# Pooled attention with a SiLU layer behind it: attention work in four groups per tile instead of five, and a second Strassen unit in tile 1

## Chip, cores and metric

The kernel runs on one core of one Trainium2 chip. The metric is the device time of one execution in microseconds. Before the change the median of three runs is 280.44 us (280.3 to 280.5). The profiled execution took 280.58 us; its span, from the first to the last instruction, is 278.7 us at a mean granted TensorE clock of 0.998. All moments below are microseconds from the start of that span.

## What is computed

```python
# q, k, v: 8 batches x 8 heads x 576 tokens x 64
k_p = k.reshape(B, H, Sp, 8, D).mean(axis=3)      # 72 pooled keys per head
v_p = v.reshape(B, H, Sp, 8, D).mean(axis=3)
scores = np.matmul(q, k_p.transpose(0, 1, 3, 2)) / np.sqrt(D)
attn = np.exp(scores - scores.max(-1, keepdims=True))
attn = attn / (attn.sum(-1, keepdims=True) + 1e-09)
x = np.matmul(attn, v_p)                          # -> 4608 tokens x 512
h = x @ w_in                                      # 512 -> 2048
out = (h / (1.0 + np.exp(-h))) @ w_out            # 2048 -> 512
```

## The kernel before

The 4608 tokens are worked off in nine tiles of 512 tokens (t = 0 to 8). Each tile has an "up" part (x by `w_in`, then SiLU) and a "down" part (the result by `w_out`). Attention for batch t + 1 is woven into the down part of tile t, in three visits (0, 1, 2), each a third of the batch's tokens. Each visit has three steps: scores with their exponentials, denominators, and numerators.

Fillers are pieces of other work that are put into the stream of matmuls at given steps:

```python
def spread(fillers, n):
    todo = sorted(fillers, key=lambda f: f[0])
    for i in range(n):
        yield i                                   # one matmul of the main stream is issued
        while todo and todo[0][0] <= i:
            todo.pop(0)[1]()
```

PSUM has eight banks: three under the tag `mm`, five under the tag `at`.

```python
banks = dict(mm=3, at=5)

def scores(b, segs):                              # four "at" banks, then four Exp on ScalarE
    sc = [ps_tile([128, 512], FP32, "at", "sc_ps")[:SP, :w] for s in range(4)]
    for g, i0, i1, cs in seg_cols(segs):
        for c in range(2):
            for s in range(4):
                nc.tensor.matmul(sc[s][:, cs], lhsT=kz[...], rhs=st["qT"][...],
                                 start=(c == 0), stop=(c == 1))
    for s in range(4):
        nc.scalar.activation(es[:, s, :], sc[s], func=AF.Exp, scale=score_scale)

def denominators(b, segs, on_dve=False):          # one "at" bank
    den_ps = ps_tile([128, 512], FP32, "at", "den_ps")
    for s in range(4):
        nc.tensor.matmul(den_ps[32*s : 32*(s+1), :w], lhsT=ones, rhs=es[:, s, :], ...)
    # ... (a variant on VectorE is left out)
    nc.scalar.activation(lnd, den_ps[:, :w], func=AF.Ln)
    nc.scalar.activation(rec, lnd, func=AF.Exp, scale=-1.0)

def numerators(b, segs, tags=("at", "at")):       # one bank of each tag named
    for c in range(2):
        nu_ps = ps_tile([128, 512], FP32, tags[c], "nu_ps")
        # 16 matmuls of vp by es
    for c in range(2):
        nc.vector.tensor_mul(out=xT[...], in0=nu[c][...], in1=rec[...])
```

The up part mixes plain groups (four matmuls of 512 columns into one `mm` bank, then Silu) with units after Strassen: seven products 1 to 7, each of four matmuls of 256 columns, in place of four plain groups. A unit has banks P and Q (`at`) and R (`mm`).

```python
# inside up():  y is the unit
if n == "2":   product(y, 2, "P", True);  nc.scalar.copy(r_sb, ps[y, "P"])
elif n == "5": product(y, 5, "Q", True);  tt(out=rr_sb, in0=ps[y, "Q"], in1=r_sb, op=ALU.add)
elif n == "1": product(y, 1, "R", True);  tt(out=t_sb, in0=ps[y, "R"], in1=rr_sb, op=ALU.subtract)
elif n == "4": product(y, 4, "P", False); hidden(y, 1, 0, ps[y, "P"])      # Silu on ScalarE
elif n == "3": product(y, 3, "Q", False); hidden(y, 0, 1, ps[y, "Q"])
elif n == "7": product(y, 7, "P", False); tt(out=c_sb[0], in0=ps[y, "P"], in1=t_sb, op=ALU.add)
elif n == "6": product(y, 6, "Q", False); tt(out=c_sb[1], in0=ps[y, "Q"], in1=t_sb, op=ALU.add)
elif n == "h": hidden(y, 0, 0, c_sb[0])
else:          hidden(y, 1, 1, c_sb[1])                                    # "s"
```

The down part of tiles 1 to 8 is one such scheme of 7 x 16 = 112 matmuls of 256 columns with three `mm` banks P, Q, R. Its order is: half of product 2, half of 5, the rest of 2, the rest of 5 (steps 0 to 31), then products 1, 4, 3, 7, 6 of 16 steps each. R is read out after product 1.

```python
ps = {n: ps_tile([128, 2, CQ], FP32, "mm", f"o_ps{n}") for n in "PQR"}
# ...
product(1, 0, KQ, cc)
tt(out=t_sb[:, cs], in0=ps["R"][:, cs], in1=rr_sb[:, cs], op=sub)
product(4, 0, KQ, cc)
copy = nc.vector.tensor_copy if last else nc.scalar.copy
copy(o_sb[1][:, cs, LO], ps["P"][:, cs])
# ... products 3, 7, 6
```

Where the attention steps stand in the down part (a = t + 1 is the batch, B = 8):

```python
sc_at, den_at, nu_at = (1, 31, 75), (31, 56, 97), (56, 97, 101)      # t > 0
for n, sg in enumerate(visits):
    f_down.append((den_at[n], lambda sg=sg: denominators(a, sg)))
    f_down.append((sc_at[n], lambda sg=sg: scores(a, sg)))
for n, sg in enumerate(visits):
    if n < 2 or not 0 < t < B - 2:
        f_down.append((nu_at[n], lambda sg=sg: numerators(a, sg)))
    if n == 0 and 1 < t < B - 1:
        f_down.append((nu_at[n], lambda: numerators(a - 1, visits[2])))
```

So numerators 2 already stood in the next tile. Tile 0 has a plain down part of 64 matmuls of 512 columns, with fillers of its own: the sums that pool `v` of batch 1 (VectorE) at steps 20 and 30, and the selection of pooled `v` (TensorE) at steps 37 and 40. The loads that it waits for are issued by GpSimd in this order: `w_out` chunks 0, 1, 2, then `v` of batch 1 in three pieces, then `w_out` chunk 3.

Of the kernel before, what the change touches and what calls it, by code (L numbers as in the profile page):

```python
# [27 lines left out]
FP32 = mybir.dt.float32  # L28
# [8 lines left out]
def kernel(  # L37
# [9 lines left out]
    nc = tc.nc  # L47

    B, H, S, D = q.shape
# [11 lines left out]
    KQ, NQ, CQ = KG // 2, NTT // 2, d_model // 2  # L61
# [29 lines left out]
    def ps_tile(shape, dtype, tag, name):  # L91
        return psum.tile(shape, dtype, tag=tag, bufs=banks[tag], name=name)
# [16 lines left out]
    o_sb = [singles.tile([128, 2, d_model], FP32, name=f"o_sb{n}") for n in range(2)]  # L109
# [130 lines left out]
    def load_slots(eng, b, name, i0, i1, half=None):  # L240
        es = slice(0, RE) if half is None else slice(half * RE // 2, (half + 1) * RE // 2)
        src = (k if name == "k" else v)[b].rearrange("h (sp p) d -> (h sp) (p d)", p=POOL)
        src = src[:, es]
        how = dict(accum_op=ALU.add) if half else {}
        tiles = row_tiles[name]
        w = es.stop - es.start
        if i0 == SLOTS:
            eng.dma_start(
                out=tiles[1][:REST, SLOTS - SA, :w], in_=src[128 * SLOTS :], **how
            )  # L250
        else:
            j = i0 // SA
            eng.dma_start(
                out=tiles[j][:, i0 - SA * j : i1 - SA * j, :w],
                in_=src[128 * i0 : 128 * i1].rearrange("(i r) e -> r i e", r=128), **how
            )
# [145 lines left out]
    def moe_tables():  # L402
        nc.scalar.preload_act_table_set("silu_and_others")
# [38 lines left out]
    def unit_x_sum(t, n):  # L442
        a, b = U_X[n]
        nc.vector.tensor_tensor(
            out=x_sum[:, U_XI[n]], in0=x_quarter(t, *a), in1=x_quarter(t, *b),
            op=ALU.subtract if n in (3, 4) else ALU.add,
        )
# [139 lines left out]
    LO, HI, FULL = slice(0, CQ), slice(CQ, 2 * CQ), slice(0, 2 * CQ)  # L587
# [30 lines left out]
    PW = 4  # L618
# [13 lines left out]
    def down_quarters(t, fillers, last=False):  # L632
        step = spread(fillers, 7 * 2 * KQ)
        ps = {
            n: ps_tile([128, 2, CQ], FP32, "mm", f"o_ps{n}") for n in "PQR"
        }
        bank = {2: "P", 5: "Q", 1: "R", 4: "P", 3: "Q", 7: "P", 6: "Q"}
        begun = set()

        def product(n, k0, k1, cs=(0, 1)):  # L640
            b = bank[n]
            for kt in range(k0, k1):
                for c in cs:
                    next(step)
                    nc.tensor.matmul(  # L645
                        ps[b][:, c, :], lhsT=left(n, kt, c), rhs=W_OUT[n][:, kt, :],
                        start=b not in begun,
                        stop=kt == k1 - 1, skip_group_check=True,
                    )
                    begun.add(b)  # L650

        add, sub = ALU.add, ALU.subtract
        tt = nc.vector.tensor_tensor
        KA = KQ // 2
        product(2, KA, KQ)
        product(5, KA, KQ)
        product(2, 0, KA)
        nc.scalar.copy(r_sb, ps["P"])
        product(5, 0, KA)
        tt(out=rr_sb, in0=ps["Q"], in1=r_sb, op=add)  # L660
        for cc in ((0,), (1,)) if last else ((0, 1),):
            cs = slice(cc[0], cc[-1] + 1)
            product(1, 0, KQ, cc)
            tt(out=t_sb[:, cs], in0=ps["R"][:, cs], in1=rr_sb[:, cs], op=sub)
            product(4, 0, KQ, cc)
            copy = nc.vector.tensor_copy if last else nc.scalar.copy
            copy(o_sb[1][:, cs, LO], ps["P"][:, cs])
            tail = last and cc == (1,)
            if tail:
                store(t, 3, LO, (nc.gpsimd,))  # L670
            product(3, 0, KQ, cc)
            nc.vector.tensor_copy(out=o_sb[0][:, cs, HI], in_=ps["Q"][:, cs])
            if tail:
                store(t, 1, HI)
            product(7, 0, KQ, cc)
            tt(out=o_sb[0][:, cs, LO], in0=ps["P"][:, cs], in1=t_sb[:, cs], op=add)
            for c in cc:
                store(t, c, LO if tail else FULL, (nc.scalar if tail else nc.sync,))
            product(6, 0, KQ, cc)
            tt(out=o_sb[1][:, cs, HI], in0=ps["Q"][:, cs], in1=t_sb[:, cs], op=add)  # L680
            for c in cc:
                if tail:
                    store(t, 3, HI, both)
                else:
                    store(t, 2 + c, FULL, (nc.gpsimd if last else nc.sync,))
        for _ in step:
            pass
# [41 lines left out]
    def load_w_out(c):  # L729
        cs = slice(c * KG // 4, (c + 1) * KG // 4)  # L730
        nc.gpsimd.dma_start(out=w_out_sb[:, cs, :], in_=w_out_r[:, cs, :])
# [43 lines left out]
    for c in range(3):  # L775
        load_w_out(c)
    load_slots(nc.gpsimd, 1, "v", 0, 3)
    load_slots(nc.gpsimd, 1, "v", 3, 4)
    load_slots(nc.gpsimd, 1, "v", 4, 5)
    load_w_out(3)  # L780

    def load_half_2(name, half):
        for i0, i1 in ((0, SA), (SA, SLOTS), (SLOTS, SLOTS + 1)):
# [9 lines left out]
    for t in range(NT):  # L793
        a = t + 1
        f_up, f_down = [], []
        if t == 0:
            GA = 11
            items = [(g, 0, HS) for g in range(GA)]
            items += [(g, HS, NTT - HS) for g in range(GA)]
            items += [(g, 0, NTT) for g in range(GA, KG)]  # L800
            f_up += [(1, lambda: denominators(0, part(0, 1), on_dve=True))]
            f_up += [(5, lambda: denominators(0, part(1, 1), on_dve=True))]
            f_up += [(13, lambda: numerators(0, part(0, 1)))]
            f_up += [(17, lambda: numerators(0, part(1, 1)))]
        else:
            G = lambda *gs: [(g, 0, NTT) for g in gs]
            if t == 1:
                items = (
                    G(12, 13, 14, 15) + [(0, "251")] + G(8) + [(0, "43")] + G(9)
                    + [(0, "7h6")] + G(10) + [(0, "s")] + G(11, 0, 1, 2, 3)  # L810
                )
            else:
                items = []
                for it in THREE[t // B].split():
                    items += [(("BCA".index(it[0])), it[1])] if it[0] in "ABC" else G(int(it[1]))
            if t == 1:
                for n in U_X:
                    f_up.append((0, lambda n=n: unit_x_sum(t, n)))
            for n in (2, 5):
                h_at = 50 if t == B else 54 if t > 1 else 45  # L820
                f_up.append((h_at, lambda n=n: hidden_sum(n, 4, 8)))
            f_up.append((56, lambda: hidden_sum(6, 4, 8)))
            for n, k0 in ((2, 0), (5, 0), (1, 4), (1, 0)):
                f_up.append((64, lambda n=n, k0=k0: hidden_sum(n, k0, k0 + 4)))
            f_down.append((33, lambda: hidden_sum(7, 0, 8)))
            f_down.append((71 if t < B else 50, lambda: hidden_sum(6, 0, 4)))

        for n, t0, f_to, at, parts in (
            (1, 0, f_down, 48, (0, PW)), (3, 0, f_down, 52, (0, PW)),
            (4, 1, f_up, 38, (0, PW)), (7, 1, f_up, 42, (0, PW)),  # L830
            (6, 1, f_up, 60, (0, PW)),
        ):
            for i in range(*parts):
                if t == t0:
                    f_to.append((at + i, lambda n=n, i=i: weight_sum(n, i)))
        if a < B:
# [44 lines left out]
            f_down.append((0, attn_tables))  # L881

            if t:
                sc_at, den_at, nu_at = (1, 31, 75), (31, 56, 97), (56, 97, 101)
            else:
                sc_at, den_at, nu_at = (1, 16, 30), (16, 30, 44), (44, 55, 56)
            for n, sg in enumerate(visits):
                f_down.append((den_at[n], lambda sg=sg: denominators(a, sg)))
                f_down.append((sc_at[n], lambda sg=sg: scores(a, sg)))

            for n, sg in enumerate(visits):
                if n < 2 or not 0 < t < B - 2:
                    f_down.append((nu_at[n], lambda sg=sg: numerators(a, sg)))
                if n == 0 and 1 < t < B - 1:
                    f_down.append((nu_at[n], lambda: numerators(a - 1, visits[2])))
        if 0 < t < B:
            for n in (4, 1, 3, 7, 6):
                f_down.append((98 if t < B - 1 else 44, lambda n=n: unit_x_sum(t + 1, n)))
        if t == 1:
            def unit_weight_tiles():  # L900
                k_w = big.tile([128, 4, 2, 256], BF16, tag="k_raw2", name="w_sum12")
# [3 lines left out]
            f_down.append((72, unit_weight_tiles))  # L905
            for i, n in enumerate(U_W):
                f_down.append((73 if i < 2 else 81, lambda n=n: unit_weight_sum(2, n)))
        moe_tables()
        up(t, f_up, items)
        if t == 0:  # L910
            down(t, f_down, [(0, 1, 2), (3,)])
# [30 lines left out]
```

The softmax here doesn't subtract the row's maximum and nothing guards it: scores larger than these inputs give would overflow.

## Time and profile before

| what | before |
|---|---|
| time, median of 3 | 280.44 us |
| span of the profiled run | 278.7 us |
| TensorE busy | 273.3 us |
| VectorE busy | 218.7 us |
| ScalarE busy | 188.4 us |
| GpSimd busy | 98.7 us |
| tile 1, from its first matmul to that of tile 2 | about 50.9 to 81.2 us |
| DMA, mean | 135 GB/s |

A busy time is the sum of the stretches in which an engine worked on something. Engines work beside each other, so the busy times don't add up to the span; an engine that is nearly always busy sets the time, and work of another engine counts only where that one waits for it. In the views quoted below PE is TensorE, PEld its loading of weights, DVE VectorE, ACT ScalarE and POOL GpSimd; L340 is line 340 of the kernel; `x16` counts instructions; and square brackets tell how long the engine had been idle and what ended that.

### The profile page before, as it was taken

The page shows a single profiled execution, that of the slowest core. Times are in us where ns is not written, and L with a number is a line of the kernel's source. Part 1 is how long each engine was busy: PE and PEld are TensorE (multiplying, and loading weights), DVE is VectorE, ACT ScalarE, POOL GpSimd, SP SyncE. Part 2 cuts the span into 40 slices and gives each one's busy share as a digit, 9 for nine tenths or more (in the row PEclk, how much of TensorE's full clock was granted, in tenths as well). Part 3 has the DMA queues.
Part 4 walks back from the last instruction along what each step waited for, and adds up shares of the span by engine and source line. Part 5 has one row for each costly group of instructions (what it writes and reads, how often), then busy time and mean ns, then how long its engine had stood idle before and what let it go on. Part 6 is the DMA issues. An engine that isn't in the chain of part 4 may idle for free.

```text
span 278.7 us, 7121 instructions
## 1 busy us (share of the span) xinstructions
PE 273.3 (98%) x2865; PEld 201.9 (72%) x2865; DVE 218.7 (78%) x413; ACT 188.4 (68%) x366; POOL 98.7 (35%) x104
## 2 busy tenths in 40 slices
PE   7999999999999999999999999999999999999995
PEld 4348444556778677867888788687877778788784
DVE  4986737889998976897689768986888588966983
ACT  1688765668577966797679757985799478326700
POOL 8745217242148430953086107961630000000001
PEclk9999999999999999999999999999999999999999
DMA  7999999896669887568865845599620041005004
GB/s 198 291 251 249 206 322 190 232 188 118 135 88 216 204 118 145 139 175 123 149 141 150 122 70 133 137 130 134 138 55 2 2 107 46 0 12 141 1 7 146
DMA packets 31312, 37.70 MB, mean 135 GB/s; under 512 B 10352, under 2 KB 22256, under 8 KB 31280
## 3 DMA queue, kind: packets, MB, share of 16 engines
q0 software_dynamic: 23920, 27.03, 52.8%
q1 hardware_dynamic: 6928, 9.58, 12.3%
q10 hardware_dynamic: 432, 0.66, 0.9%
q8 instruction: 22, 0.36, 0.6%
q14 instruction: 10, 0.08, 0.1%
HBM read 36.70 MB, written 9.44 MB: 166 GB/s over the span
## 4 chain that ended last, share of the span: by engine, by line
PE 81%; DMA 12%; POOL 2%; DVE 2%; issue 1%; DVEq 0%; POOLq 0%
PE o_psP L645 16%; PE o_psQ L645 16%; PE hp_ps L537 12%; PE u_psP L477 10%; PE u_psQ L477 10%; DMA w_in_sb<-in_moe_w_in_dram 6%; DMA w_out_sb<-in_moe_w_out_dram 6%; PE o_psR L645 5%; PE u_psR L477 3%; PE sc_ps L340 3%; PE nu_ps L384 2%; PE den_ps L358 2%; DVE w_sum L623 1%; POOL q_bf L133 1%; DVE xT L393 1%
## 5 line engine op out<-in xcount | busy, mean ns | idle before, releaser
L645 PEld LDWEIGHTS <-h_sum 128*128 128x128 bf16 x640 | 60.6, 98 | 11.9 <-DVE h_sum L605 1.5
L537 PE MATMUL hp_ps<-xT,w_in_sb 128*128 128x512 bf16 (+3 forms) x284 | 54.1, 334 | 0.1
L605 DVE TENSOR_TENSOR h_sum<-h_T 128x1024 bf16<-128x1024 bf16 (+1 forms) x72 | 49.7, 742 | 0.0
L477 PEld LDWEIGHTS <-w_sum 128*128 128x128 bf16 x440 | 43.1, 98 | 7.8
L348 ACT ACTIVATE es<-sc_ps 72x384 bf16<-72x384 f32 (+1 forms) x100 | 39.1, 470 | 8.5 <-PE sc_ps L340 8.3
L543 ACT ACTIVATE h_T<-hp_ps 128x512 bf16<-128x512 f32 (+2 forms) x67 | 33.8, 524 | 11.5 <-PE hp_ps L537 10.5
L537 PEld LDWEIGHTS <-w_in_sb 128*128 128x128 bf16 x284 | 27.1, 98 | 17.1 <-issue 1.1
L485 ACT ACTIVATE h_T<-c_sb 128x512 bf16<-128x512 f32 x44 | 27.5, 628 | 3.1 <-DVE c_sb L509 2.4
L393 DVE TENSOR_TENSOR xT<-nu_ps,rec 128x384 bf16<-128x384 f32 (+1 forms) x50 | 24.0, 532 | 4.4 <-PE nu_ps L384 4.3
L645 PEld LDWEIGHTS <-h_T 128*128 128x128 bf16 x256 | 24.1, 98 | 4.5 <-issue 0.9
L549 POOL DMA_DIRECT2D out_dram<-o_sb x2 | 1.2, 618 | 68.2 <-issue 67.4
L367 ACT ACTIVATE lnd<-den_ps 128x384 f32<-128x384 f32 (+1 forms) x23 | 11.1, 484 | 19.9 <-PE den_ps L358 19.9
L190 POOL TENSOR_TENSOR raw<-raw 72x1024 f32<-72x1024 f32 x10 | 23.6, 2365 | 0.1
L500 DVE TENSOR_TENSOR t_sb<-u_psR,rr_sb 128x512 f32<-128x512 f32 x22 | 15.2, 692 | 7.0 <-PE u_psR L477 5.5
L494 ACT COPY r_sb<-u_psP 128x512 f32<-128x512 f32 x22 | 12.9, 584 | 10.0 <-PE u_psP L477 8.7
L263 DVE TENSOR_TENSOR raw<-raw 128x384 f32<-128x384 f32 (+3 forms) x20 | 12.4, 618 | 9.3 <-DMA raw<-in_v_dram 4.9
L477 PEld LDWEIGHTS <-w_in_sb 128*128 128x128 bf16 x176 | 16.9, 98 | 2.3
L645 PE MATMUL o_psP<-w_out_sb,h_sum 128*128 128x256 bf16 x128 | 17.6, 273 | 0.0
L497 DVE TENSOR_TENSOR rr_sb<-u_psQ,r_sb 128x512 f32<-128x512 f32 x22 | 14.9, 679 | 2.9 <-ACT r_sb L494 1.6
L509 DVE TENSOR_TENSOR c_sb<-u_psP,t_sb 128x512 f32<-128x512 f32 x22 | 15.1, 688 | 2.7 <-PE u_psP L477 1.0
L512 DVE TENSOR_TENSOR c_sb<-u_psQ,t_sb 128x512 f32<-128x512 f32 x22 | 15.1, 687 | 2.4 <-PE u_psQ L477 2.3
L645 PE MATMUL o_psQ<-w_sum,h_sum 128*128 128x256 bf16 x128 | 16.7, 273 | 0.0
(84 smaller groups left out, 507.3 us busy)
## 6 DMA issues: line engine op xcount, KB each, us to landing
out_dram<-o_sb SPq DMA_DIRECT2D x128, 64.0 KB, 1.7
raw<-in_k_dram POOLq DMA_DIRECT2D x10, 576.0 KB, 7.9
raw<-in_v_dram POOLq DMA_DIRECT2D x10, 576.0 KB, 7.9
q_bf<-in_q_dram POOLq DMA_DIRECT2D x6, 576.0 KB, 10.5
w_in_sb<-in_moe_w_in_dram POOLq DMA_DIRECT2D x8, 256.0 KB, 8.3
w_out_sb<-in_moe_w_out_dram POOLq DMA_DIRECT2D x4, 512.0 KB, 13.3
raw<-in_v_dram POOLq DMA_DIRECT2D x2, 768.0 KB, 11.1
raw<-in_k_dram POOLq DMA_DIRECT2D x1, 768.0 KB, 10.6
```

The source lines that it names most:

```text
L190: nc.gpsimd.tensor_add(out=raw[:, :, : 2 * D], in0=raw[:, :, : 2 * D], in1=raw[:, :, 2 * D :])
L348: nc.scalar.activation(es[:, s, :], sc[s], func=AF.Exp, scale=score_scale)
L393: nc.vector.tensor_mul(out=xT[:, 2 * g0 + c : 2 * (g0 + ng - 1) + c + 1 : 2, cols], in0=nu[c][:, :w].rearrange("r (g n) -> r g n", g=ng), ...
L477: nc.tensor.matmul(ps[y, bank][:, u, :], lhsT=w[:, kk, 128 * u : 128 * (u + 1)], rhs=x[:, kk, :], start=first and u == 0 and kk == 0, stop ...
L485: nc.scalar.activation(h_T[:, g : g + 2, j * NQ : (j + 1) * NQ], src, func=AF.Silu)
L500: tt(out=t_sb, in0=ps[y, "R"], in1=rr_sb, op=ALU.subtract)
L509: tt(out=c_sb[0], in0=ps[y, "P"], in1=t_sb, op=ALU.add)
L512: tt(out=c_sb[1], in0=ps[y, "Q"], in1=t_sb, op=ALU.add)
L537: nc.tensor.matmul(hp_ps[:, r0:r1], lhsT=w_in_sb[:, kk, g * 128 : (g + 1) * 128], rhs=xT[:, kk, x0 : x0 + r1 - r0], start=(kk == 0), stop= ...
L543: nc.scalar.activation(h_T[:, g, n0 : n0 + n], hp_ps[:, :n], func=AF.Silu)
L605: nc.vector.tensor_tensor(out=h_sum[n][:, ks, :], in0=quarter(*a, ks), in1=quarter(*b, ks), op=op)
L645: nc.tensor.matmul(ps[b][:, c, :], lhsT=left(n, kt, c), rhs=W_OUT[n][:, kt, :], start=b not in begun, stop=kt == k1 - 1, skip_group_check= ...
```

## The change

It regroups the attention steps of tiles 1 to 5 so that TensorE leaves the main stream four times instead of five. Numerators 1 move from step 97 to 79.5, just ahead of scores 2 (step 80), and since the five `at` banks do not suffice there, one of their two tiles takes an `mm` bank, that of the third sum R, which is free by then. Denominators 2 move into the next tile, ahead of denominators 0 (step 33). Tile 1 gets a second Strassen unit in place of four plain groups; to make room, weight sums for the down part are computed earlier (many of them in tile 0), for which the last `w_out` chunk is loaded ahead of two pieces of `v`. The sums of x for the next tile move from step 98 to 92, the table load for tile 1 from the start of tile 1 into tile 0, and in the last tile one copy goes from VectorE to ScalarE.

```diff
-            n: ps_tile([128, 2, CQ], FP32, "mm", f"o_ps{n}") for n in "PQR"
+            n: ps_tile([128, 2, CQ], FP32, "mm", f"o_ps{n}") for n in "RPQ"
@@ down part
-            copy = nc.vector.tensor_copy if last else nc.scalar.copy
-            copy(o_sb[1][:, cs, LO], ps["P"][:, cs])
+            nc.scalar.copy(o_sb[1][:, cs, LO], ps["P"][:, cs])
@@ loads
     load_slots(nc.gpsimd, 1, "v", 0, 3)
+    load_w_out(3)
     load_slots(nc.gpsimd, 1, "v", 3, 4)
     load_slots(nc.gpsimd, 1, "v", 4, 5)
-    load_w_out(3)
@@ tile 1, up part: digits are products, (0, ...) the first unit, (1, ...) the second
-                    G(12, 13, 14, 15) + [(0, "251")] + G(8) + [(0, "43")] + G(9)
-                    + [(0, "7h6")] + G(10) + [(0, "s")] + G(11, 0, 1, 2, 3)
+                    G(12, 13, 14, 15) + [(0, "25143"), (1, "2"), (0, "7"), (1, "5")]
+                    + [(0, "6h"), (1, "1"), (0, "s")] + G(0) + [(1, "43")] + G(1)
+                    + [(1, "7h6")] + G(2) + [(1, "s")] + G(3)
@@ weight sums for the down part: product, tile, part, step, pieces (PW = 4)
             (1, 0, f_down, 48, (0, PW)), (3, 0, f_down, 52, (0, PW)),
-            (4, 1, f_up, 38, (0, PW)), (7, 1, f_up, 42, (0, PW)),
-            (6, 1, f_up, 60, (0, PW)),
+            (6, 0, f_down, 8, (0, PW)), (4, 0, f_down, 12, (0, 2)),
+            (7, 0, f_down, 14, (0, 2)), (4, 1, f_up, 8, (2, PW)), (7, 1, f_up, 10, (2, PW)),
@@ attention in the down part
-                sc_at, den_at, nu_at = (1, 31, 75), (31, 56, 97), (56, 97, 101)
+                sc_at, den_at, nu_at = (1, 33, 80), (33, 56, 97), (56, 79.5, 101)
+                if t == B - 2:
+                    sc_at, nu_at = (1, 33, 75), (56, 97, 101)
+            later = 0 < t < B - 2
+            if 1 < t < B - 1:
+                f_down.append((den_at[0], lambda: denominators(a - 1, visits[2])))
             for n, sg in enumerate(visits):
-                f_down.append((den_at[n], lambda sg=sg: denominators(a, sg)))
+                if n < 2 or not later:
+                    f_down.append((den_at[n], lambda sg=sg: denominators(a, sg)))
                 f_down.append((sc_at[n], lambda sg=sg: scores(a, sg)))
             for n, sg in enumerate(visits):
-                if n < 2 or not 0 < t < B - 2:
-                    f_down.append((nu_at[n], lambda sg=sg: numerators(a, sg)))
+                tags = ("mm", "at") if later and n == 1 else ("at", "at")
+                if n < 2 or not later:
+                    f_down.append(
+                        (nu_at[n], lambda sg=sg, tags=tags: numerators(a, sg, tags))
+                    )
                 if n == 0 and 1 < t < B - 1:
                     f_down.append((nu_at[n], lambda: numerators(a - 1, visits[2])))
@@ sums of x for the next tile
-                f_down.append((98 if t < B - 1 else 44, lambda n=n: unit_x_sum(t + 1, n)))
+                f_down.append((44 if t == B - 1 else 98 if t == B - 2 else 92, lambda n=n: unit_x_sum(t + 1, n)))
@@ table loads
-        moe_tables()
+        if t != 1:
+            moe_tables()
+        if t == 0:
+            f_down.append((46, moe_tables))
```

## The prediction

> **What bounds the kernel now.** I read the busy times first, then the chain that ended last, then stretches of the time line.
>
> ```profile
> PE 273.3 (98%) x2865; PEld 201.9 (72%) x2865; DVE 218.7 (78%) x413; ACT 188.4 (68%) x366; POOL 98.7 (35%) x104
> PE 81%; DMA 12%; POOL 2%; DVE 2%; issue 1%; DVEq 0%; POOLq 0%
> ```
>
> TensorE (PE) is busy 98% of the span, and the chain is TensorE for 81% of it; its DMA part ends at 42.66 us, with the last chunk of `w_out`. So the time is what TensorE executes plus every moment it waits, and nothing else on any other engine counts unless TensorE waits for it. A busy share hides short waits of a tenth of a microsecond, so I looked at the order of work on TensorE in tile 2, and at ScalarE (ACT) beside it:
>
> ```profile
> 98.08 0.35 PE L358 MATMUL den_ps<-es,ones 72*32 72x384 bf16 x4
> 98.36 0.54 PE L340 MATMUL sc_ps<-qT,kz 32*72 32x192 bf16 x16
> 98.55 0.49 ACT L367 ACTIVATE lnd<-den_ps 128x384 f32<-128x384 f32 x1 [0.36 <-PE den_ps L358]
> 98.83 1.92 PE L645 MATMUL o_psR<-w_sum,h_sum 128*128 128x256 bf16 x16
> 99.08 0.52 ACT L368 ACTIVATE rec<-lnd 128x384 f32<-128x384 f32 x1
> 99.51 1.60 ACT L348 ACTIVATE es<-sc_ps 72x384 bf16<-72x384 f32 x4
> ...
> 101.66 0.35 PE L358 MATMUL den_ps<-es,ones 72*32 72x384 bf16 x4
> 101.83 0.83 PE L384 MATMUL nu_ps<-es,vp 72*32 72x192 bf16 x32
> 102.60 0.94 PE L645 MATMUL o_psP<-w_sum,h_T 128*128 128x256 bf16 x7
> ```
>
> Columns: start and length in us, engine, line. Four denominator matmuls take 0.28 us until the scores can start (98.08 to 98.36), yet when the next matmul has the same small shape they take only 0.17 (101.66 to 101.83). So about 0.10 us is lost each time TensorE goes from one array shape to another. Second reading: ACT starts the logarithm 0.47 us after the denominators start (98.08 to 98.55) and needs 0.49.
>
> Third, tile 0, where the DMA part of the chain ends:
>
> ```profile
> 38.96 1.55 DVE L263 TENSOR_TENSOR raw<-raw 128x768 f32<-128x768 f32 x2 [4.92 <-DMA raw<-in_v_dram]
> 40.82 1.14 DVE L263 TENSOR_TENSOR raw<-raw 128x512 f32<-128x512 f32 x2
> 42.71 0.10 PEld L572 LDWEIGHTS <-h_T 128*128 128x128 bf16 x1 [0.38 <-issue]
> 43.14 0.34 PE L303 MATMUL v_ps<-v,shifts 128*128 128x64 bf16 x6
> 43.99 0.33 PE L303 MATMUL v_ps<-v,shifts 128*128 128x64 bf16 x6
> ```
>
> TensorE stops before 42.71, until the last `w_out` chunk is there: seven 512-wide matmuls start from 41.36, at 0.216 us each by the matmuls around them, so the next was due near 42.45 to 42.5. It loses about 0.25 us. VectorE (DVE) had waited 4.92 us for `v`.
>
> **What the Trainium skill says.** "TensorEngine Tiling (Array Packing)", Key Properties: changing the tiling mode drains the array. The trace agrees and prices it at about 0.10 us. "TensorE: Matmul & The Clock Gate", Back-to-back issue gap: N/2.4 + 2.5 ns between warm matmuls, so 109 ns at 256 columns and 216 at 512; the chain shows eight 256-wide ones in 0.87 us (109 ns) and four 512-wide ones in 0.86 to 0.87 (216 ns). The same section gives 131 ns as a sustained figure at 512; this trace does not reach that. "Perfetto Trace Analysis", Optimization Strategy: a bubble that repeats on the engine that should be full can mean too few buffers. No run of the kernel before shows such a bubble in tiles 2 to 6; I expect the change to make one. "ScalarE: Activation LUTs", What ACT_TABLE_LOAD costs: 1283 ns for the load; the trace has 1.28 us. TensorE does not wait for it here.
>
> **The change part by part.**
>
> (a) Second unit in tile 1. Four plain groups of four 512-wide matmuls, 16 x 0.216 = 3.46 us, become seven products of four 256-wide ones, 28 x 0.109 = 3.05. Saved: 0.41 us on the path. The price is on DVE: four more sums of 0.69 us in a stretch in which the first unit's sums, the copies of `kz` and three transposes stand in the queue. The new unit's products 4 and 7 share a bank, so product 7 waits for the Silu of product 4, and the ACT queue has the first unit's last Silu ahead of it, which waits for DVE's sum. Queueing the measured durations (rr 0.69, t 0.69, kz 0.5, transposes 1.2, c 2 x 0.69, rr 0.69, c 0.69, t 0.69) I find ACT some 0.3 to 0.6 us too late once. I book +0.3, an estimate. Eight of the twelve weight sums that tile 1 ran leave it (0.35 each in a row), four stay early in it; that roughly pays for the four new sums, and I book -0.1 for a short wait on a hidden sum at the start of tile 1's down part.
>
> (b) Fewer switches of shape. Before, a tile has groups at steps 1, 31, 56, 75, 97; that is 2+3+2+2+2 = 11 switches. After, at 1, 33, 56 and 79.5/80: 2+3+2+3 = 10. Tiles 1 to 5: 5 x 0.10 = 0.5 us saved. The matmuls themselves are as many as before.
>
> (c) Denominators 2 in the next tile, at step 33 just ahead of denominators 0 and scores 1. Here I expect the price. The attention banks (tag `at`) are five. In the program of the kernel before, a tile takes at its first use the bank that was freed first. At step 31 that is one bank for the denominators and the four of scores 0 for scores 1: nobody waits. At step 33 six tiles are wanted: denominators 2 take the one idle bank, denominators 0 and the first three scores tiles take the four of scores 0, and the fourth scores tile gets the bank of denominators 2, which is free only when ACT has taken its logarithm. With T the start of the group, scores would start at T + 0.17 + 0.28 = T + 0.45. The logarithm ends at T + 0.47 + 0.49 = T + 0.96, and a semaphore costs about 0.05 (a DVE product ends at 51.32, its matmul starts at 51.37): T + 1.01. So TensorE stops for 0.56 us. It happens in tiles 2 to 6 (the condition is 1 < t < 7): 5 x 0.56 = 2.8 us. ACT then does two logarithms, two exponentials and four score exponentials, ending near T + 4.0; TensorE reaches step 56 at about T + 4.05, so no second wait there.
>
> (d) The last `w_out` chunk ahead of two `v` pieces. The wait before 42.71 goes (-0.25). But `v` now ends where `w_out` ended, near 42.66; DVE needs 42.29 - 40.82 = 1.47 us for the last sums, so they are ready at about 44.15, and the second selection of `v`, which without the wait would come at 43.74, starts at 44.2 instead of 43.99. All later work of tile 0 is chained to it. Net +0.2.
>
> (e) The last tile's copies on ACT. DVE did a 0.41 us copy twice in a full queue, and TensorE waited some 0.18 and 0.06 us near 269 and 270 for the two banks. Saved: 0.2.
>
> (f) The order "RPQ" changes nothing if a bank is taken at first use, as P is still used first; the table load at step 46 and the earlier x sums move work on engines for which TensorE does not wait.
>
> Sum: -0.41 + 0.3 - 0.1 - 0.5 + 2.8 + 0.2 - 0.2 = +2.1, so 280.4 + 2.1 = about 282.4.
>
> **The rivals.** First: no bank wait in (c). Then the sum is -0.7, and with a tile 1 that flows freely -1.0: 279.4 to 279.8. For it speaks that the group was placed with care and that the five tiles had no other wait; against it, that five banks for six tiles leave no other choice unless banks are taken in another order than the program before shows. Second: the banks P, Q, R are fixed by the order of their names. Then the first product of the down part, P, takes the bank of the last but one plain group, whose Silu in tile 2 ends at 94.3, while TensorE wants it at 93.92. That costs 0.4 us in tiles 2 to 8, some 3 us more, and the time would be near 285. Third: VectorE becomes the bound of tile 1 (27.0 of 30.3 us busy there before). Each further sum that comes late costs 0.7, so up to +1.
>
> **Range and chances.** The centre is 282.4. The lower end has the first rival, 279.6; the upper one has (c) plus a poor tile 1 and a little of the second rival, 284.2. Two per cent is 5.6 us: a gain of that size has no source here (all savings together are 1.5), a loss would need (c) and the second rival both.
>
> **What would show it.** Right: in tiles 2 to 6, TensorE idle for about 0.55 us within the scores of step 33, after their third matmul, until the first logarithm of the pair ends; tiles of 29.2 us from start to start where the chain now has 28.73 (82.20 to 110.94); `v` waited for in tile 0 and `w_out` no longer; tile 1 about as long as before. Wrong: scores of step 33 that start and end without a gap (the first rival), a gap before the first matmul of each down part (the second), or tile 1 more than 0.7 us off.

## The result, and the profile after

| what | before | after |
|---|---|---|
| time, median of 6 runs each | 280.47 us | 282.33 us |
| ratio to before, 95% interval | | 1.0061 [1.0048, 1.0075] |
| span of the profiled run | 278.7 us | 280.6 us |
| first matmul of tile 1 | 50.94 | 51.48 |
| first plain group of tiles 2, 3, 6 in the chain | 82.20, 110.94, 197.18 | 82.35, 111.44, 198.74 |
| the same of tiles 7, 8 | 226.46, 251.33 | 228.64, 253.51 |
| start of the last sum on VectorE | 275.59 | 277.55 |

The changed kernel is 0.6% slower: less than 2%, but the interval lies clear of 1. The busy times and the chain by engine on its page:

```profile
PE 273.7 (98%) x2877; PEld 203.7 (73%) x2877; DVE 221.1 (79%) x415; ACT 189.2 (67%) x369; POOL 98.3 (35%) x104
PE 78%; DMA 12%; DVE 4%; POOL 2%; ACT 1%; issue 1%; POOLq 0%; DVEq 0%
```

TensorE is busy 98% as before, and these shares alone would tell nothing. But the chain has got 4% of VectorE (2% before) and 1% of ScalarE (none before): TensorE now waits for them at a few places. The differences of the marks in the table say where (a plain group of tiles 2 to 8 lies about 1 us after the first matmul of its tile). Tile 0 is 0.54 us longer, tile 1 (50.94 to 82.20, now 51.48 to 82.35) 0.39 shorter, tiles 2 to 5 together 1.41 longer (114.98 to 116.39), tile 6 0.62 longer, tile 7 the same, the last tile 0.22 shorter. That adds up to the 1.96 us between the two last sums.

**Tiles 2 to 6.** The time line of tile 2, at the place that the prediction quoted of before:

```profile
98.44 0.51 PE L358 MATMUL den_ps<-es,ones 72*32 72x384 bf16 x8
98.84 0.49 ACT L367 ACTIVATE lnd<-den_ps 128x384 f32<-128x384 f32 x1 [0.50 <-PE den_ps L358]
98.88 0.28 PE L340 MATMUL sc_ps<-qT,kz 32*72 32x192 bf16 x3
99.36 0.52 ACT L368 ACTIVATE rec<-lnd 128x384 f32<-128x384 f32 x1
99.38 0.50 PE L340 MATMUL sc_ps<-qT,kz 32*72 32x192 bf16 x13 [0.22 <-ACT lnd L367]
99.79 0.47 ACT L367 ACTIVATE lnd<-den_ps 128x384 f32<-128x384 f32 x1
99.81 1.70 PE L645 MATMUL o_psR<-w_sum,h_sum 128*128 128x256 bf16 x14
100.73 1.60 ACT L348 ACTIVATE es<-sc_ps 72x384 bf16<-72x384 f32 x4
```

The 16 matmuls of the scores are cut into 3 and 13. The fourth, the first one into the fourth scores bank, starts at 99.38, right after the logarithm of denominators 2 has ended (98.84 + 0.49 = 99.33). Before, the main stream went on 0.47 us after the scores began (98.36 to 98.83); now it takes 0.93 (98.88 to 99.81). So the stop costs 0.46 us, and the same 0.93 stands in each of tiles 2 to 6. From start to start, tile 2 went from 28.73 to 29.09 us: +0.36, which is the stop less one switch of shape.

**Tile 0.**

```profile
38.61 1.55 DVE L263 TENSOR_TENSOR raw<-raw 128x768 f32<-128x768 f32 x2 [0.48 <-DMA raw<-in_v_dram]
42.67 1.15 DVE L263 TENSOR_TENSOR raw<-raw 128x512 f32<-128x512 f32 x2 [2.12 <-DMA raw<-in_v_dram]
42.80 0.34 PE L303 MATMUL v_ps<-v,shifts 128*128 128x64 bf16 x6
44.07 0.41 DVE L310 CAST vp<-v_ps 72x256 bf16<-72x256 f32 x1
44.53 0.33 PE L303 MATMUL v_ps<-v,shifts 128*128 128x64 bf16 x6 [0.75 <-DVE vp L310]
```

The last `v` sums begin at 42.67 instead of 40.82, since two pieces of `v` now come after the last `w_out` chunk. The second selection of `v` starts at 44.53 instead of 43.99, though the first one starts 0.34 us earlier (42.80 for 43.14). It does not wait for the sums but for the copy of the first half out of the bank (L310): both selections write one bank, and that copy stands behind the sums in VectorE's queue and ends at 44.48.

**Tile 1.** The chain runs here through VectorE and ScalarE (start, length, engine, line):

```profile
58.38 0.94 DVE qT L159 x3
59.40 0.65 DVE c_sb L509
60.05 0.60 DVE rr_sb L497
60.65 0.61 DVE c_sb L512
61.28 0.63 ACT h_T L485
61.91 0.48 ACT h_T L543
62.40 0.50 ACT h_T L485
62.94 0.60 PE u_psP L477 x4
```

The last line is product 7 of the second unit. It wants bank P, from which ScalarE reads the Silu of product 4 (the third ACT line); that waits its turn behind the first unit's last Silu (the first ACT line), which waits for its sum (L512), before which VectorE did three transposes. Four 512-wide matmuls had begun at 61.70 and take 0.86, so product 7 was due at 62.56: a stop of about 0.38 us. The up part of tile 1 lasts 14.11 us (51.48 to 65.59), against 14.07 before (50.94 to 65.01): 0.41 us of matmuls less by the prediction's sum, and nothing gained in this part.

### The profile page after: what moved, and what is told of

It reads as the page before. It is cut to its first block, busy times and chain, and to the rows that moved or that the text cites. A ratio compares the mean times of both kernels' runs of the same rounds, so it can differ in the third digit from the quotient of the medians.

```text
span 280.6 us, 7165 instructions
## 1 busy us (share of the span) xinstructions
PE 273.7 (98%) x2877; PEld 203.7 (73%) x2877; DVE 221.1 (79%) x415; ACT 189.2 (67%) x369; POOL 98.3 (35%) x104
## 4 chain that ended last, share of the span: by engine, by line
PE 78%; DMA 12%; DVE 4%; POOL 2%; ACT 1%; issue 1%; POOLq 0%; DVEq 0%
PE o_psP L645 16%; PE o_psQ L645 15%; PE u_psP L477 11%; PE hp_ps L537 10%; PE u_psQ L477 10%; DMA raw<-in_v_dram 9%; PE o_psR L645 5%; DMA raw<-in_k_dram 3%; PE u_psR L477 3%; PE sc_ps L340 3%; PE nu_ps L384 2%; PE den_ps L358 1%; DVE w_sum L623 1%; DVE xT L393 1%; ACT lnd L367 1%
## 5 line engine op out<-in xcount | busy, mean ns | idle before, releaser
L477 PEld LDWEIGHTS <-w_sum 128*128 128x128 bf16 x460 | 45.0, 98 | 8.4 <-issue 0.5
L537 PE MATMUL hp_ps<-xT,w_in_sb 128*128 128x512 bf16 (+3 forms) x268 | 50.5, 332 | 0.1
L543 ACT ACTIVATE h_T<-hp_ps 128x512 bf16<-128x512 f32 (+2 forms) x63 | 31.7, 520 | 10.3 <-PE hp_ps L537 7.2
L537 PEld LDWEIGHTS <-w_in_sb 128*128 128x128 bf16 x268 | 25.6, 98 | 15.3 <-issue 1.1
L485 ACT ACTIVATE h_T<-c_sb 128x512 bf16<-128x512 f32 x46 | 28.8, 628 | 4.5 <-DVE c_sb L509 3.1
L500 DVE TENSOR_TENSOR t_sb<-u_psR,rr_sb 128x512 f32<-128x512 f32 x23 | 15.9, 692 | 8.8 <-PE u_psR L477 7.2
L477 PEld LDWEIGHTS <-w_in_sb 128*128 128x128 bf16 x184 | 17.6, 98 | 2.4
L497 DVE TENSOR_TENSOR rr_sb<-u_psQ,r_sb 128x512 f32<-128x512 f32 x23 | 15.7, 682 | 3.2 <-ACT r_sb L494 1.8
L512 DVE TENSOR_TENSOR c_sb<-u_psQ,t_sb 128x512 f32<-128x512 f32 x23 | 15.8, 687 | 2.4 <-PE u_psQ L477 2.3
L509 DVE TENSOR_TENSOR c_sb<-u_psP,t_sb 128x512 f32<-128x512 f32 x23 | 15.8, 687 | 2.3 <-PE u_psP L477 1.0
L645 PE MATMUL o_psR<-w_sum,h_sum 128*128 128x256 bf16 x128 | 16.7, 273 | 0.0
```

Source lines behind the costliest of these rows:

```text
L477: nc.tensor.matmul(ps[y, bank][:, u, :], lhsT=w[:, kk, 128 * u : 128 * (u + 1)], rhs=x[:, kk, :], start=first and u == 0 and kk == 0, stop ...
L485: nc.scalar.activation(h_T[:, g : g + 2, j * NQ : (j + 1) * NQ], src, func=AF.Silu)
L537: nc.tensor.matmul(hp_ps[:, r0:r1], lhsT=w_in_sb[:, kk, g * 128 : (g + 1) * 128], rhs=xT[:, kk, x0 : x0 + r1 - r0], start=(kk == 0), stop= ...
L543: nc.scalar.activation(h_T[:, g, n0 : n0 + n], hp_ps[:, :n], func=AF.Silu)
L645: nc.tensor.matmul(ps[b][:, c, :], lhsT=left(n, kt, c), rhs=W_OUT[n][:, kt, :], start=b not in begun, stop=kt == k1 - 1, skip_group_check= ...
```

## The experiments

The theory after this reading has three causes: a bank in tiles 2 to 6 (five stops of 0.46 us), the order of the loads in tile 0, and the queue of VectorE in tile 1. All times are medians; each ratio is to the kernel before on the same chip. Different groups of runs were made on different chips; where a few tenths count, only runs beside each other are compared. Three runs (the transposes later, the second unit taken back and the copy alone, each the first time) had one execution at a granted clock of 0.56 to 0.95, which is left out of their medians; in the first of them it is the profiled one.

### Denominators 2 at another step, with a sixth bank

```diff
-            if 1 < t < B - 1:
-                f_down.append((den_at[0], lambda: denominators(a - 1, visits[2])))
+                if n == 1 and 1 < t < B - 1:          # in the loop, after denominators 1
+                    f_down.append((den_at[1], lambda: denominators(a - 1, visits[2])))
...
-                    f_down.append((nu_at[n], lambda: numerators(a - 1, visits[2])))
+                    f_down.append((nu_at[n], lambda: numerators(a - 1, visits[2], ("mm", "at"))))
```

> The changed kernel, but denominators 2 of the last batch stand at step 56 beside denominators 1, and one of numerators 2's two tiles takes an mm bank, so that at no step six attention tiles share five banks. Same work, same number of switches of shape. Theory (the 0.46 us stop within the scores of step 33 is the wait for the bank of denominators 2): the stop goes in tiles 2 to 6, 5 x 0.46 = 2.3 us, 280.0 us. Rival (ScalarE's two logarithms and two exponentials ahead of the score exponentials hold TensorE up, whatever the bank): the work only moves to step 56 and a stop appears there or at step 80, 281.5 to 282.3 us.

Measured: 280.13 us, ratio 0.9989 [0.9981, 0.9998], 2.2 us under the changed kernel's first measurement. In its tile 2 the scores run through, and eight denominator matmuls stand together at step 56:

```profile
99.25 0.35 PE L358 MATMUL den_ps<-es,ones 72*32 72x384 bf16 x4
99.53 0.54 PE L340 MATMUL sc_ps<-qT,kz 32*72 32x192 bf16 x16
100.00 1.70 PE L645 MATMUL o_psR<-w_sum,h_sum 128*128 128x256 bf16 x14
...
102.61 0.51 PE L358 MATMUL den_ps<-es,ones 72*32 72x384 bf16 x8
102.95 0.83 PE L384 MATMUL nu_ps<-es,vp 72*32 72x192 bf16 x32
```

A tile lasts 28.63 us (83.16 to 111.79 in the chain). That is 0.46 under the changed kernel and 0.10 under the kernel before: one switch of shape saved. But this moves ScalarE's work as well as the bank.

### The same ScalarE work at the same group, another bank

```diff
-                f_down.append((den_at[0], lambda: denominators(a - 1, visits[2])))
+                f_down.append((31, lambda: denominators(a - 1, visits[2], tag="mm")))
...
-                sc_at, den_at, nu_at = (1, 33, 80), (33, 56, 97), (56, 79.5, 101)
+                sc_at, den_at, nu_at = (1, 31, 80), (31, 56, 97), (56, 79.5, 101)
```

Tile 6 has the same 31 for 33; `denominators` takes the tag of its bank as an argument.

> The changed kernel, but the group of denominators 2, denominators 0 and scores 1 stands at step 31 in place of 33, and denominators 2 take the mm bank that R takes right after it. ScalarE does the same instructions in the same order as in the changed kernel; only the bank differs. Theory (bank): scores 1 have five fresh banks and run through; R's first matmul wants its bank about 0.92 us after the group starts, and the logarithm that frees it ends at about 0.90 to 0.95, so a stop of at most 0.05 us remains: 280.0 to 280.3 us. Rival (ScalarE's order, not the bank): still 282.3 us.

Measured: 280.96 us, ratio 1.0022 [1.0012, 1.0033]. Neither theory has it right. The time line of tile 2:

```profile
98.46 0.51 PE L358 MATMUL den_ps<-es,ones 72*32 72x384 bf16 x8
98.90 0.54 PE L340 MATMUL sc_ps<-qT,kz 32*72 32x192 bf16 x16
99.40 1.91 PE L645 MATMUL o_psR<-w_sum,h_sum 128*128 128x256 bf16 x16
...
102.22 0.50 PE L358 MATMUL den_ps<-es,ones 72*32 72x384 bf16 x4
102.40 0.98 PE L384 MATMUL nu_ps<-es,vp 72*32 72x192 bf16 x32
```

The cut in the scores is gone: from their start to the main stream it is 0.50 us, for 0.47 before. The fourth scores matmul starts at 98.91, while the logarithm of denominators 2 ends only at 99.35 (98.86 + 0.49): with another bank, TensorE no longer waits for it. So the bank was the cause of that stop. The program of the changed kernel fits this: in each of tiles 2 to 6 its fourth scores tile has the bank of denominators 2. But the denominators of step 56 and the numerators after them now take 1.09 us (102.22 to 103.31, the next line of the main stream), and 0.94 before (101.66 to 102.60): the fourth of these denominator matmuls starts only when the last of the score exponentials is done, at about 102.34. ScalarE's two further functions ahead of the exponentials are the rival's mechanism, worth 0.15 us here. A tile lasts 28.80 us (82.58 to 111.38). Of what was to be had, 29.09 - 28.63 = 0.46, the bank gave 0.29 by itself, and the rest turned into the wait for ScalarE.

### Denominators 2 alone

```diff
-                f_down.append((den_at[0], lambda: denominators(a - 1, visits[2])))
+                f_down.append((16, lambda: denominators(a - 1, visits[2])))
```

> The changed kernel with denominators 2 alone at step 16, far from any other attention step. Bank theory: five fresh banks are there at step 33, so the stop of 0.46 us goes in five tiles (-2.3), but the group stands alone and costs two switches of shape, 0.2 us each time (+1.0): 281.0 us. If switches cost nothing: 280.0. If the bank is not the cause: 283.3.

Measured: 281.43 us, ratio 1.0031 [1.0019, 1.0043]. The group alone, and the scores of step 33 behind it:

```profile
96.89 0.35 PE L358 MATMUL den_ps<-es,ones 72*32 72x384 bf16 x4
97.17 0.94 PE L645 MATMUL o_psP<-w_out_sb,h_sum 128*128 128x256 bf16 x7
...
99.40 0.54 PE L340 MATMUL sc_ps<-qT,kz 32*72 32x192 bf16 x16
99.87 1.38 PE L645 MATMUL o_psR<-w_sum,h_sum 128*128 128x256 bf16 x11
```

No stop (99.40 to 99.87, 0.47 us). A tile lasts 28.85 us (81.61 to 110.46 from first matmul to first matmul): 0.24 under the changed kernel and 0.22 over the run with denominators 2 at step 56. The expectation was -0.46 + 0.20 = -0.26. So a group on its own costs about 0.2 us for its two switches, which fits a price of 0.10 for one. The median lies 0.4 us above the expected 281.0, though by their length the five tiles gain 5 x 0.24 = 1.2 us; in this profile tile 1 starts at 51.78, for 51.48 in the changed kernel's, and the next experiment shows why such starts differ.

### The last `w_out` chunk after `v` again

```diff
     load_slots(nc.gpsimd, 1, "v", 0, 3)
-    load_w_out(3)
     load_slots(nc.gpsimd, 1, "v", 3, 4)
     load_slots(nc.gpsimd, 1, "v", 4, 5)
+    load_w_out(3)
```

> The changed kernel with the last w_out chunk loaded after all of v again, as before. Theory: tile 0 loses the stop of 0.75 us before the second selection of v and gets back the stop of 0.25 us for w_out; the first matmul of tile 1 comes 0.5 us earlier, 281.8 us. Rival (weight sums moved into tile 0 hold VectorE up, not the order of the loads): 282.3 us, the selection is as late as in the changed kernel.

Measured: 281.90 us, ratio 1.0052 [1.0035, 1.0069]. Its tile 0:

```profile
41.23 1.14 DVE L263 TENSOR_TENSOR raw<-raw 128x512 f32<-128x512 f32 x2
42.89 0.59 PE L572 MATMUL o_ps<-w_out_sb,h_T 128*128 128x512 bf16 x2 [0.56 <-DMA w_out_sb<-in_moe_w_out_dram]
43.32 0.34 PE L303 MATMUL v_ps<-v,shifts 128*128 128x64 bf16 x6
44.17 0.34 PE L303 MATMUL v_ps<-v,shifts 128*128 128x64 bf16 x6
```

The weight sums that the change put into tile 0 are still there, and the last `v` sums still begin at 41.23: the order of the loads made the delay, not the sums. TensorE waits for `w_out` again, and the selection follows without a stop. The first matmul of tile 1 comes at 51.12, for 51.48 in the changed kernel's profile. The interval overlaps that of the changed kernel, so the time alone doesn't prove the gain; the profiles of the runs with the early chunk have tile 1 start between 51.48 and 52.31, those with the late one between 50.59 and 51.22. The early ones follow one rule: in all eight that can be compared the second selection starts 1.86 us after the last `v` sums begin, and tile 1 starts 6.95 us after that selection. Those sums begin between 42.67 and 43.50, when `v` lands; so it is the landing of `v` that sets the start of tile 1 there.

### The three transposes later

```diff
-            q_at = [4, 14, 4, 8] if t > 1 else [24, 25, 26, 2] if t else [82, 84, 86, 88]
+            q_at = [4, 14, 4, 8] if t > 1 else [36, 37, 38, 2] if t else [82, 84, 86, 88]
```

> The changed kernel with the three transposes of tile 1's up part at steps 36 to 38 in place of 24 to 26. Theory: the transposes stand ahead of the first unit's two last sums, ScalarE's Silu on them holds up the Silu of the second unit's product 4, and product 7 waits for that: with the transposes later the stop of 0.37 us goes, 281.95 us. Rival (the second unit's sums are late for another reason, or the transposes now hold up the hidden sums at the end of the up part): 282.3 us.

Measured: 282.15 us, ratio 1.0063 [1.0050, 1.0077], about as slow as the changed kernel on another chip (282.33). Its profile can't be compared, so the kernel was run again beside the changed kernel itself:

> The changed kernel itself once more, beside the next three on one chip, so that differences of a few tenths of a microsecond can be told. Expected as at first: 282.3 us, 1.9 us over the kernel before.

Measured: 282.83 us, ratio 1.0084 [1.0071, 1.0096]; half a microsecond over the first measurement of the same kernel.

> The transposes of tile 1's up part at steps 36 to 38 once more, since the first profile of it was of a throttled execution. Theory (transposes ahead of the first unit's last sums): the up part of tile 1 goes from 14.10 us to 13.7, and the time is 0.4 us under the changed kernel beside it. Rival: the up part stays at 14.1.

Measured: 282.30 us, ratio 1.0067 [1.0054, 1.0080], 0.53 us under the changed kernel beside it; the intervals overlap. Product 7 of the second unit and the matmuls before it:

```profile
61.93 1.19 DVE L159 STREAM_TRANSPOSE qT<-q_bf 128x288 f32<-128x288 f32 x3
62.12 1.03 PE L537 MATMUL hp_ps<-xT,w_in_sb 128*128 128x512 bf16 x4
62.26 0.59 ACT L485 ACTIVATE h_T<-u_psP 128x512 bf16<-128x512 f32 x1
62.98 0.60 PE L477 MATMUL u_psP<-x_sum,w_sum 128*128 128x256 bf16 x4
```

It starts 0.86 us after the plain group (62.12 to 62.98), without a stop. The up part of tile 1 lasts 13.68 us (51.90 to 65.58), 0.4 less than with the transposes early. The cause is shown by the trace; the time agrees with it.

### The second unit taken back

The diff is the line with `"25143"` in the change, reversed. The first run:

> The changed kernel with the second unit of tile 1 taken back (four plain groups, in the order of before); the weight sums stay where the change put them. Theory: the unit saves 0.41 us of matmuls and costs the stop of 0.37 us at its product 7, so taking it back changes nothing: 282.3 to 282.4 us. Rival (the stop would come without the unit too, from the full VectorE queue): 282.7 us.

Measured: 282.98 us, ratio 1.0088 [1.0073, 1.0102]. This was 0.65 us over the changed kernel on another chip, where no difference was expected, so it was repeated beside it:

> The second unit of tile 1 taken back, once more: its up part lasted 14.06 us with four plain groups and 14.10 with the unit, which makes no difference, but the first time measured was 0.7 us over the changed kernel's on another chip. Theory (unit and stop cancel): within 0.2 us of the changed kernel beside it. Rival (the unit saves time elsewhere): 0.4 us or more over it.

Measured: 283.09 us, ratio 1.0096 [1.0082, 1.0110], 0.26 us over the control beside it, with intervals that overlap. Its up part of tile 1 lasts 14.07 us (51.57 to 65.64), with the unit 14.10 (52.31 to 66.41). So in this part unit and stop cancel. From the first matmul of tile 1 to the end of the last sum, the profile without the unit has 226.56 us and the control's 226.48; the up part of tile 2 is 0.13 us longer without it (12.88 for 12.75). After that, the last store took 2.22 us from its issue to its landing, for 1.69 in the control. So the unit gains about 0.1 us by the profiles. The longer store is there in both profiles without the unit (2.09 and 2.22); whether it belongs to this kernel stays open.

### The copy in the last tile alone

```diff
-            copy = nc.vector.tensor_copy if last else nc.scalar.copy
-            copy(o_sb[1][:, cs, LO], ps["P"][:, cs])
+            nc.scalar.copy(o_sb[1][:, cs, LO], ps["P"][:, cs])
```

This one edits the kernel before.

> The kernel before with one thing of the change alone: in the last tile ScalarE copies bank P out in place of VectorE. Theory: the two short stops near the end (0.18 and 0.06 us) go: 280.3 us, 0.2 us under the kernel before. Rival (the end is set by the last store, not by TensorE): no difference.

Measured: 280.45 us, ratio 0.9998 [0.9990, 1.0006]. The interval holds both no gain and the 0.2 us expected, so the time can't tell them apart. The last down part is 0.22 us shorter on TensorE in its profile (12.14 for 12.36 us from its first to its last matmul), as in the changed kernel. The last sum ends at 275.46 here and at 276.01 before, and the spans are 278.7 both. Most of the earlier moment comes from tile 0 (tile 1 starts at 50.59, for 50.94), and the last store took 2.26 us from its issue to its landing, for 1.69 before. That is not what the change does in general. In the changed kernel's profile the last store took 1.68 us, and from the first matmul of the last down part to the end it is 15.50 us, for 15.74 before: there the gain reached the end. Of the thirteen profiles that can be compared, ten have 1.7 us for the last store and three 2.1 to 2.3; why stays open.

### All three repairs

Denominators 2 at step 56 with an `mm` bank, the last chunk after `v`, and the transposes at 36 to 38.

> The changed kernel with three repairs: denominators 2 at step 56 with an mm bank for numerators 2, the last w_out chunk after v, and the three transposes of tile 1's up part at steps 36 to 38 in place of 24 to 26. If the three causes add up: -2.3 for the bank, -0.5 for the loads, -0.4 for the stop of product 7 of the second unit in tile 1: 279.1 us, faster than the kernel before by 1.3 us. Rival (the stops hide one another, or move the next wait into their place): 279.8 us or more.

Measured: 279.11 us, ratio 0.9955 [0.9940, 0.9970]. And beside the control:

> All three repairs once more, beside the changed kernel on one chip: 3.2 us under it by the sum of the three causes (2.3 + 0.5 + 0.4), 279.1 us; 1.3 us under the kernel before. If the repairs overlap: 2.5 us under it or less.

Measured: 279.06 us, ratio 0.9956 [0.9943, 0.9970], 3.8 us under the changed kernel beside it and 1.4 us (0.4%) under the kernel before. The 3.8 is more than the sum of 3.2, but this control was half a microsecond slower than the first measurement, and the gain from the loads is not a fixed one. The part that does not depend on loads adds up to the hundredth. From the first matmul of tile 1 to the end of the last sum, the profiles have 226.49 us for the changed kernel, 224.18 with the bank alone repaired, 226.10 with the transposes alone, and 223.79 with all three: 2.31 + 0.39 = 2.70. The idea of the change was sound, and three waits hid it.

## Why the prediction was right

The mechanism was right: the main price is a wait for a bank, where and when the prediction said. That the predicted 282.4 us and the measured 282.33 agree to a tenth is luck, for the steps behind them are less exact. The wait was booked 0.5 us too long and the loads 0.34 too short, with opposite signs. And the terms of the prediction's sum make +2.09, from 280.4 to 282.5 and not 282.4.

- **(c) The bank in tiles 2 to 6** was the decisive step, and right in kind and place: the stop is after the third scores matmul and ends with the first logarithm. The size was 0.46 us, not 0.56, in all five tiles 2.3 and not 2.8. The working's wait runs from the first scores matmul to the fourth. It came out at 0.50 (98.88 to 99.38): ACT started its logarithm 0.40 us after the denominators, not 0.47, and ended it 0.05 us before the matmul, as booked. Of these 0.50 TensorE lost 0.46 in the group as a whole. ScalarE's exponentials being just in time at step 56 was right too: where the bank no longer delayed TensorE, they were 0.15 us late.
- **(b) Switches.** 0.10 us each, seen twice: 28.73 to 28.63 us with the stop gone, and +0.22 for a group by itself. The prediction's "as many matmuls as before" missed a shift: denominators 2 left tile 1, and tile 6 has two such groups. That is 0.17 us less in tile 1 and 0.17 more in tile 6, nothing in the sum; it explains why tile 6 lost 0.62 us (0.46 + 0.17).
- **(a) Second unit.** Predicted -0.41 and a stop of 0.3 to 0.6 with a booking of +0.3; the stop is 0.38 us, at the product named and through the queue named. All of it went with the transposes moved. Tile 1 as a whole came out 0.39 us shorter: 0.10 from the switch, 0.17 from the denominators that moved away, and about 0.1 from the wait for a hidden sum, which is gone as booked (eight matmuls of product 5 took 0.97 us, 66.45 to 67.42, and now 0.88, 67.03 to 67.91).
- **(d) The loads** were the poorest step. Booked +0.2; tile 1 started 0.54 us later in the first profile and up to 1.4 us later in others with the early chunk. The step failed in taking the second selection to wait for the `v` sums alone, at 44.2. It waits for the copy of the first half too, which the sums push back in VectorE's queue: 0.33 us more (44.53). And the landing of `v` differs between executions: the sums began at 42.67 in one profile and at 43.50 in that of the same program later, where the prediction had one moment, 42.66. Its reading of the wait for `w_out` holds, but of the seven matmuls that it counts from 41.36 five ran before the wait, and these five give its 42.45.
- **(e) The last tile.** TensorE gained 0.22 us as predicted, and in the changed kernel's profile the gain reached the end of the span. The run with the copy alone is too coarse to confirm it in the time.
- **(f)** With the names in the order "PQR" again, the built program has the same instructions on the same banks: the order of names does nothing. The second rival, a stop before the first product of each down part, does not appear; the down part of tile 2 begins 12.75 us after the tile does before the change and 12.76 after it.

The rival without a bank wait is refuted by the cut scores and by their whole run in the three kernels that gave a fresh bank. The rival of a late VectorE in tile 1 was right to the extent of one stop of 0.38 us, for which the centre had booked 0.3.

## What to carry to other kernels

When groups of small matmuls are merged to save switches, count the buffers that the merged group wants at once: one tile too many for the pool makes the engine wait for a reader on another engine, and that wait (0.46 us here) can exceed the switch it saves (0.10). Two halves of one buffer can act as one buffer for waits: here the writing of the second half began 0.05 us after the copy of the first, queued behind long sums, had ended. (By the traces; no run gave the second half a bank of its own.) And a repair that frees the bound engine by some tenths can make the next engine late: with the bank alone changed, 0.15 us of the 0.46 came back as a wait for ScalarE, and with another place for the denominators nothing did. So undo suspected causes one at a time and then all at once.

## What was not expected of the hardware

The same program differs between executions by where its loads land: the sums on the last pieces of `v` began at 42.67 us in one profile of the changed kernel and at 43.50 in another, and its medians, 282.33 and 282.83 us, lie apart by more than most terms of the working. Between tile 1 and the last sum, by contrast, the profiles of the same program agree to 0.01 us (226.49 and 226.48). After the last sum it took 2.6 us to the end in ten profiles and 3.0 to 3.2 in the other three.
